# Banded attention in tiles of 32 queries by 64 keys, feeding a top-1 mixture of experts

## The chip, the cores and the metric

The kernel runs on one core of a Trainium2 chip. A core has a matrix engine (PE, TensorE; its weight loads are listed apart as PEld), three engines for elementwise work (DVE = VectorE, ACT = ScalarE, POOL = GpSimd), a queue engine that issues most DMAs (SP = SyncE) and 16 DMA engines. The metric is the device time of one execution in microseconds (us); lower is better.

## The reference

```python
B, H, S, D = 8, 8, 576, 64
scores = scale * q @ k.transpose(0, 1, 3, 2)
rel = pos[:, None] - pos[None, :]
mask_plain = (rel >= 0) & (rel < 32)                       # heads 0-3
mask_dil = (rel >= 0) & (rel < 128) & (rel % 4 == 0)       # heads 4-7
attn = softmax(where(mask, scores, -1e9))
x = (attn @ v).transpose(0, 2, 1, 3).reshape(4608, 512)
# top-1 mixture of 8 experts, gate logits with a bias per modality
logits = x @ w_gate + modality_bias[modality_id]
e_idx, gate_w = argmax(logits), softmax(logits)[e_idx]
out[e_idx == e] = gate_w * (relu(x @ w1[e]) @ w2[e])       # w1: 512x1024, w2: 1024x512
```

Every query looks at 32 keys: heads 0 to 3 at the last 32 positions, heads 4 to 7 at every fourth of the last 128. Everything is float32.

## The kernel before

**Two halves.** The first is attention with routing, the second the experts. Attention goes over 8 batches of 5 steps each, 40 steps (`s`, with `b, n = s // 5, s % 5`). Heads 0 to 3 are "plain" (`kd == 0`); heads 4 to 7 are "dilated" (`kd == 1`) and their positions are sorted into four classes of 144, so that their mask becomes a band of 32 too. Steps `n` = 0 and 1 take dilated tiles, 3 and 4 plain ones, 2 the rest of both and half as much.

**A tile before** is 64 queries (`TQ`) by 96 keys (`KW = TQ + WIN`); a step holds two tiles one above the other in the 128 partitions, for 2 values of `x`, 2 of `g` and 2 of `a`: 8 units of 128 rows. What a step does is spread over five turns of the loop, so that one turn `s` contains `scores` of step s (PE: `qT` x `kT` into the PSUM tile `pss`; DVE adds the mask at L397 and takes the row maximum at L399; POOL subtracts it in `sm`), `exp` of step s-1 (ACT, L404), a copy of values `shift_v` (ACT, L150 or L152), `attend` of step s-2 (PE, L418, into `po`), `logits` of s-4 (PE, L470 or L473 and L475), `normalize` of s-2 (DVE, L425 to L432), `turn` of s-3 (PE transposes at L456, ACT copy `ux`), a piece of `qk_chunks` for coming steps (PE transposes of q and k at L353, ACT copy into `qkT` at L355), `probsT` of s-1 (PE transposes of the probabilities at L410, ACT copy `pT` at L412), and `keep` of s-2 (DMA of the result `x_sb` to `x_dram`).

**Values** lie in three buffers `vw` of 96 partitions: 64 partitions of a block of 64 positions, and above them the 32 positions before, which `shift_v` copies from the block before.

**Order.** PE, DVE, ACT and SP run exactly in the order in which the loop issues (`manual_schedule`), and POOL in the order of its wrapper `pool`; each engine waits by itself for what its next instruction needs. SP issues, in that same order, the loads of q, k and v for the next batch, the stores of `keep` and the loads for the experts. `background` runs the routing of a finished batch (`gating`, the scatter of token numbers into `table` by POOL's indirect DMAs) in small pieces between the steps, on a time `state['t']` of 9 ticks a batch. After batch 2, four expert slots are already full: `fetch_slot` has SP read their token numbers into `idt`, and POOL gathers their rows of `x_dram` into `xr` (indirect DMAs, four to a slot) at ticks that a list names.

**PSUM** has 8 banks: `po` 2, `pss` 2 and a ring of two tiles of 2 banks (`banks()`), which `qk_chunks`, `probsT`, `turn` and later the experts' first product take by turns. When `state['go']` is set, near the end of attention, `pss` is given up and the experts start: 18 slots of 256 tokens and one of 128, each with 8 pieces of w1 (L948) and w2 (L928), split on ACT and DVE into a high and a low part (L896, L897).

## Time and profile before

| | |
|---|---|
| Median of 3 runs | 685.75 us (683.57 to 688.63) |
| The profiled execution | 687.67 us; its span, first to last instruction, 685.9 us |
| Mean granted PE clock | 0.971 |
| Busy share of the span | PE 94%, PEld 82%, DVE 67%, ACT 62%, POOL 36% |
| First scores (L391) to last | 11.7 us to about 229 us |
| Experts | from about 238 us to 677 us |

A row of the timeline is start, length, engine, line, operation, tiles, count, and in brackets the idle time before it with what ended it. A row of groups gives count, then busy us and mean ns of one, then idle time before. A float32 matmul stands as two records in the trace where it isn't a transpose.

### The profile page before, as it was taken

Reading aid. Unit: us, or ns where it says so; the run is one execution under the profiler, and the core shown is the slowest. Engines: PE = TensorE matmul, PEld = TensorE weight load, DVE = VectorE, ACT = ScalarE, POOL = GpSimd, SP = SyncE. Lnnn points to the kernel's source line nnn. Section 1 sums busy time; section 2 is a strip of 40 time slices with the busy share of each in tenths; the row PEclk is TensorE's granted clock in tenths of the full one; section 3 lists DMA queues with packets and bytes.
Section 4 is the critical chain, followed back from the end, with each engine's and each line's share of the span. In section 5 each row is a group of like instructions: output and inputs, shape, how many; then the busy total and the mean of one; then the engine's idle time right before and its main releaser. Section 6 shows DMA issues by size and latency. Waiting matters only on the chain. (4 is left out here: it accounts for less than half of the span.)

```text
span 685.9 us, 17663 instructions
## 1 busy us (share of the span) xinstructions
PE 644.7 (94%) x6481; PEld 563.9 (82%) x6481; DVE 456.7 (67%) x967; ACT 428.7 (62%) x749; POOL 248.1 (36%) x300
## 2 busy tenths in 40 slices
PE   7899988996989898999999999999999999999994
PEld 4777877875777787899999999999999999999983
DVE  4666565772657666866776677667766776677652
ACT  3777968675787554566566656655666566656552
POOL 7333554544656553333242331333313231311110
PEclk9899999998999799999999999999999999999998
DMA  9886976868598843593963337823323335831550
GB/s 207 218 188 168 189 178 153 184 170 185 125 187 214 265 97 97 145 248 105 267 175 93 94 109 213 216 78 110 103 83 78 108 117 151 240 92 63 154 145 14
DMA packets 133630, 103.32 MB, mean 151 GB/s; under 512 B 67648, under 2 KB 111698, under 8 KB 133540
## 3 DMA queue, kind: packets, MB, share of 16 engines
q1 hardware_dynamic: 124964, 82.31, 47.5%
q0 software_dynamic: 8176, 19.26, 9.8%
q8 instruction: 52, 0.85, 0.5%
q10 hardware_dynamic: 400, 0.59, 0.3%
q14 instruction: 38, 0.31, 0.2%
HBM read 127.52 MB, written 29.39 MB: 229 GB/s over the span
## 5 line engine op out<-in xcount | busy, mean ns | idle before, releaser
L897 DVE TENSOR_TENSOR w2l<-w2q,w2h 128x512 fp32r<-128x512 f32 x152 | 104.9, 690 | 42.2 <-ACT w2h L896 33.9
L317 POOL DMA_INDIRECT xr<-x_dram,idt x74 | 81.9, 1107 | 109.7 <-DMA x_slot<-xr 76.9
L948 PE MATMUL pt<-xh,w1l 128*128 128x256 f32 (+1 forms) x420 | 119.3, 284 | 1.5 <-DVE w1l L897 1.5
L948 PE MATMUL pt<-xh,w1h 128*128 128x256 f32 (+1 forms) x420 | 119.5, 285 | 0.7 <-DVE hl L955 0.7
L948 PE MATMUL pt<-xl,w1h 128*128 128x256 f32 (+1 forms) x420 | 119.2, 284 | 0.0
L928 PE MATMUL py<-w2h,hh 128*128 128x512 f32 x296 | 117.8, 398 | 0.0
L928 PE MATMUL py<-w2h,hl 128*128 128x512 f32 x296 | 117.0, 395 | 0.0
L928 PE MATMUL py<-w2l,hh 128*128 128x512 f32 x296 | 116.2, 393 | 0.0
L954 ACT ACTIVATE hh<-pt 128x256 fp32r<-128x256 f32 (+1 forms) x105 | 39.8, 379 | 119.0 <-PE pt L948 119.0
L317 POOL DMA_INDIRECT out_dram<-ys,idt x37 | 39.5, 1069 | 205.5 <-ACT ys L931 129.6
L897 DVE TENSOR_TENSOR w1l<-w1q,w1h 128x512 fp32r<-128x512 f32 x152 | 104.2, 685 | 1.3 <-ACT w1h L896 1.3
L896 ACT CAST w1h<-w1q 128x512 fp32r<-128x512 f32 x152 | 94.5, 622 | 1.2 <-DVE hl L955 0.9
L896 ACT CAST w2h<-w2q 128x512 fp32r<-128x512 f32 x152 | 93.1, 612 | 0.0
L948 PEld LDWEIGHTS pt<-xh,w1h 128*128 128x128 f32 x420 | 80.9, 193 | 6.4 <-DVE hl L955 0.9
L948 PEld LDWEIGHTS pt<-xl,w1h 128*128 128x128 f32 x420 | 80.9, 193 | 3.9
L948 PEld LDWEIGHTS pt<-xh,w1l 128*128 128x128 f32 x420 | 80.8, 192 | 2.0 <-DVE w1l L897 2.0
L317 POOL TENSOR_TENSOR sm<-sm,nmx 128x768 f32<-128x768 f32 (+1 forms) x40 | 53.7, 1343 | 77.4 <-DVE den L425 36.6
L955 DVE SCALAR_TENSOR_TENSOR hl<-pt,hh 128x256 fp32r<-128x256 f32 (+1 forms) x105 | 43.7, 417 | 54.7 <-ACT hh L954 54.6
L397 DVE TENSOR_TENSOR sm<-pss,masks 128x768 f32<-128x768 f32 (+1 forms) x40 | 34.9, 873 | 57.4 <-PE pss L391 49.5
L928 PEld LDWEIGHTS py<-w2l,hh 128*128 128x128 f32 x296 | 55.8, 188 | 13.3
L418 PE MATMUL po<-vw,pT 96*64 96x65 f32 (+1 forms) x1216 | 56.7, 234 | 8.6 <-DVE t L540 3.5
L418 PEld LDWEIGHTS po<-vw,pT 96*64 96x64 f32 (+1 forms) x1216 | 46.2, 141 | 19.6 <-ACT ex L528 4.3
(181 smaller groups left out, 1220.4 us busy)
## 6 DMA issues: line engine op xcount, KB each, us to landing
w2q<-in_moe_w_dram SPq DMA_DIRECT2D x76, 512.0 KB
w1q<-in_moe_w_dram SPq DMA_DIRECT2D x152, 256.0 KB
x_slot<-xr SPq DMA_DIRECT2D x18, 512.0 KB
xg<-x_slot SPq DMA_DIRECT2D x72, 128.0 KB
x_dram<-x_sb SPq DMA_DIRECT2D x32, 256.0 KB
st<-in_k_dram SPq DMA_DIRECT2D x8, 576.0 KB
st<-in_k_dram SPq DMA_DIRECT2D x32, 144.0 KB
st<-in_q_dram SPq DMA_DIRECT2D x32, 144.0 KB
```

What stands on the lines that cost most here:

```text
L317: ins = tc.keep_in_program_order(getattr(nc.gpsimd, name)(*args, **kw))
L397: nc.vector.tensor_tensor(out=sm.rearrange("p (a x) w -> p a x w", a=2), in0=pss[:, :, 0:2 * nx * KW].rearrange("p a (x w) -> p a x w", w=KW),
L418: nc.tensor.matmul(out=po[r0:r0 + nr, x, o:o + D + 1], lhsT=self.pT[:, 2 * self.nx * a + 2 * x + g, r0:r0 + nr], rhs=self.vts[kd][:, blk, ...
L896: nc.scalar.copy(out=hi, in_=raw)
L897: nc.vector.tensor_tensor(out=lo, in0=raw, in1=hi.bitcast(F32), op=ALU.subtract)
L928: nc.tensor.matmul(out=py[u], lhsT=ht[:, us], rhs=wt, start=(f + n == 0), stop=(f + n == FC + 1))
L948: nc.tensor.matmul(out=ph, lhsT=wt[:, c, :], rhs=xt[:, c, 0:cols], start=(c + i == 0), stop=(c + i == KC + 1))
L954: nc.scalar.activation(out=hh, in_=ph, func=AF.Relu)
L955: nc.vector.scalar_tensor_tensor(out=hl, in0=ph, scalar=0.0, in1=hh.bitcast(F32), op0=ALU.max, op1=ALU.subtract)
```

## The change

Tiles become 32 queries by 64 keys. Four of them lie above one another in the 128 partitions and two (`x` = 0, 1) side by side, so that `sm` is 4 units of 128 x 128 instead of 8 of 128 x 96, one transpose of `probsT` turns the probabilities of two units, and the two halves of its 128 output partitions are multiplied with values of 64 partitions each. A step has 32 score matmuls of 32 x 64 and 32 of attend instead of 16 and 16. The value buffers get 128 partitions (a second, shifted copy, for tiles that start in the middle of a block), which doubles the shifts: four a batch stay on ACT, four go to DVE. `probsT` moves ahead of `normalize` and `turn`. The PSUM ring is replaced by tiles of their own: `pc` (2 banks) for `qk_chunks`, `pt` (1) for `probsT`, `px` (1) for `turn`; the experts get `ph0` and `ph1`, and `pt` and `px` after attention. After the first two steps, only n = 2 has two chunks of `qk_chunks`. The stores of `keep` become two for each full step, v has four small loads more a batch, and the loads of q and k come at n = 1 and n = 3 instead of n = 0 and n = 4. The ticks at which POOL gathers the first two slots change.

```diff
-KW = TQ + WIN
+KW = 2 * WIN
+VO = D + 2
+VBLK = 20
...
-    ring = [pspool.tile([P, 2, 512], F32, name=f"pt{i}") for i in range(2)]
+    pt = pspool.tile([P, 512], F32, name="pt")
+    px = pspool.tile([P, 512], F32, name="px")
...
+    pss, pc = (spool.tile([P, 2, 512], F32, name=name) for name in ("pss", "pc"))
+    ring, turn = [], [0]
...
-    vws = [avw.tile([KW, 4 * (HT + 1), VB], F32, name=f"vw{i}") for i in range(3)]
+    vws = [avw.tile([P, VBLK, VB], F32, name=f"vw{i}") for i in range(3)]
...
+    def shift_v(copy, b, kd, low, n):
+
+        t = vw(b, kd).rearrange("p k d -> p (k d)")
+        w = (2 + 2 * kd) * VB * low
+        r0 = WIN * (1 - low)
+        copy(out=t[r0:r0 + WIN, 8 * VB * n + w:8 * VB * (n + 1) + w], in_=t[P - WIN - r0:P - r0, 8 * VB * n:8 * VB * (n + 1)])
...
         def scores(self):
...
+                            to = pss[WIN * c:WIN * (c + 1), a, kw * g + KW * x:kw * g + KW * (x + 1)]
+                            nc.tensor.matmul(out=to, lhsT=qT[kd][ar, h, WIN * j:WIN * (j + 1)], rhs=kT[kd][ar, h, WIN * j:WIN * j + KW], start=True, stop=True)
...
         def probsT(self):
-            ptt = banks()
-            nx = self.nx
-            for j in range(4 * nx):
-                nc.tensor.transpose(out=ptt[0:KW, j // 4, P * (j % 4):P * (j % 4 + 1)], in_=self.sm[:, j, :], identity=ident)
-            self.pT = awk.tile([KW, 8, P], F32, name="pT", bufs=1)[:, 0:4 * nx]
-            nc.scalar.copy(out=self.pT.rearrange("p (k j) c -> p k (j c)", j=4), in_=ptt[0:KW, 0:nx])
+            kw = self.nx * KW
+            for h in range(4):
+                nc.tensor.transpose(out=pt[0:kw, P * h:P * (h + 1)], in_=self.sm[:, h], identity=ident)
+            self.pT = awk.tile([P, 4, P], F32, name="pT", bufs=1)[0:kw]
+            nc.scalar.copy(out=self.pT.rearrange("p h c -> p (h c)"), in_=pt[0:kw])
 
         def attend(self):
...
+            for a in range(2):
+                for g in range(2):
+                    for x, c, kd, j, hh in self.js:
+                        r = slice(TQ * x, TQ * (x + 1))
...
+                        nc.tensor.matmul(out=po[WIN * c:WIN * (c + 1), x, o:o + D + 1], lhsT=self.pT[r, 2 * a + g, WIN * c:WIN * (c + 1)],
+                                         rhs=self.vts[kd][r, blk, (D + 1) * a:(D + 1) * (a + 1)], start=True, stop=True)
...
-            t0 = (b + 2) * 9 + 6
-            yield from together(first_rows(0, (t0, t0 + 1, t0 + 9, t0 + 10, t0 + 11, t0 + 12, t0 + 14)), first_rows(1, (t0 + 18, t0 + 19, t0 + 26, t0 + 27)), first_slot())
+            t0 = (b + 2) * 9 + 12
+            yield from together(first_rows(0, (t0, t0 + 1, t0 + 9, t0 + 10, t0 + 11, t0 + 12, t0 + 14)), first_rows(1, (t0 + 14, t0 + 15, t0 + 18, t0 + 19)), first_slot())
...
+    SHIFTS = (((on_dve, 1, 0, 0),), ((on_dve, 1, 1, 0),), ((on_act, 1, 0, 1), (on_dve, 1, 1, 1)), ((on_act, 0, 1, 1),), ((on_act, 0, 0, 0), (on_dve, 0, 1, 0)))
...
         if 0 <= s - LAG:
             steps[s - LAG].logits()
+        if 0 <= s - 1 < NST:
+            steps[s - 1].probsT()
         if 0 <= s - 2 < NST:
             steps[s - 2].normalize()
...
-        if 0 <= s - 1 < NST:
-            steps[s - 1].probsT()
...
-            if n == 0:
+            if n == 1:
                 state['k', 0] = load_one(b + 1, 0, k)
                 state['qk', b + 1, 0] = load_one(b + 1, 0, q), state['k', 0]
-            elif n == 1:
                 state['v', b + 1, 1] = load_v(b + 1, 1)
+            elif n == 3 and b + 2 < B:
+                state['qk', b + 2, 1] = load_qk(b + 2, 1)
             elif n == 4:
-                if b + 2 < B:
-                    state['qk', b + 2, 1] = load_qk(b + 2, 1)
                 state['v', b + 1, 0] = load_v(b + 1, 0)
...
-    ring.append(po)
+    ring += [pt, px]
```

How this moves the order is shown at three places. The first is PE in one whole step, n = 0 of the second batch, from its scores up to the next step's; the sizes are those of one output, and xN counts equal instructions. Before:

```order
L391 MATMUL pss<-qkT_102 64x96 x16
L418 MATMUL po<-vw_104,pT 64x65 x16
L470 MATMUL po<-ux,wgs 32x2x64 x4
L456 MATMUL pt_80<-ident,x_sb 128x128 x2
L353 MATMUL pt_79<-ident,st 128x96 x8
L410 MATMUL pt_80<-ident,sm 96x128 x8
L353 MATMUL pt_79<-ident,st 128x96 x8
```

and now (L378 is scores, L406 attend, L469 logits, L395 `probsT`, L455 `turn`, L345 `qk_chunks`):

```order
L378 MATMUL pss<-qkT_103 32x64 x32
L406 MATMUL po<-vw_104,pT 32x65 x32
L469 MATMUL po<-ux,wgs 32x2x64 x4
L395 MATMUL pt<-ident,sm 128x128 x4
L455 MATMUL px<-ident,x_sb 128x128 x2
L345 MATMUL pc<-ident,st 128x96 x8
```

The probabilities' transposes have moved ahead of `turn` and are half as many, the matmuls of scores and attend are twice as many, and one of this step's chunks has gone to the next step.

The second place is POOL in the middle of the fifth batch's scatter, where the first slot's rows are gathered; the first row is the subtraction of step 25 (counted from 0). Before:

```order
L317 TENSOR_TENSOR sm<-sm,nmx 128x768
L560 DMA table<-pay,dst 41472x3
L317 DMA xr<-x_dram_85,idt 128x256
L317 DMA xr<-x_dram_86,idt 128x256
L560 DMA table<-pay,dst 41472x3
L317 TENSOR_TENSOR sm<-sm,nmx 128x768
L560 DMA table<-pay,dst 41472x3 x2
```

and now, from the same subtraction on:

```order
L310 TENSOR_TENSOR sm<-sm,nmx 128x512
L559 DMA table<-pay,dst 41472x3 x2
L310 TENSOR_TENSOR sm<-sm,nmx 128x512
L559 DMA table<-pay,dst 41472x3
L310 DMA xr<-x_dram_86,idt 128x256
L559 DMA table<-pay,dst 41472x3
L310 TENSOR_TENSOR sm<-sm,nmx 128x4x64
L310 DMA xr<-x_dram_87,idt 128x256
```

The first gather stands one subtraction later, and the second one more.

The third place is SP over one batch of stores and loads, from the last store of plain tiles on. Before:

```order
L446 DMA x_dram_85<-x_sb 128x2x256
L141 DMA vw_104<-in_v_dram 64x4x128 x2
L141 DMA vw_104<-in_v_dram 16x4x128
L141 DMA vw_104<-in_v_dram 48x4x128
L141 DMA vw_104<-in_v_dram 64x4x128
L141 DMA vw_104<-in_v_dram 32x4x128
L449 DMA x_dram_86<-x_sb 128x2x256 x2
L439 DMA x_dram_85<-x_sb 64x256
L442 DMA x_dram_86<-x_sb 32x2x128 x2
L121 DMA st<-in_k_dram 96x4x384
L121 DMA st<-in_q_dram 96x4x384
L137 DMA vw_105<-in_v_dram 64x9x64 x4
```

and now, from the stores of dilated tiles on to the loads that follow the next plain ones:

```order
L445 DMA x_dram_87<-x_sb 64x4x128 x4
L124 DMA st<-in_k_dram 96x4x384
L124 DMA st<-in_q_dram 96x4x384
L432 DMA x_dram_86<-x_sb 64x256
L435 DMA x_dram_87<-x_sb 32x2x128 x2
L141 DMA vw_106<-in_v_dram 64x8x64 x4
L144 DMA vw_106<-in_v_dram 64x2x64
L145 DMA vw_106<-in_v_dram 32x2x64
L144 DMA vw_106<-in_v_dram 64x2x64
L145 DMA vw_106<-in_v_dram 32x2x64
L440 DMA x_dram_86<-x_sb 4x32x256 x4
L121 DMA st<-in_k_dram 96x6x64 x4
```

A batch has 35 DMAs on SP instead of 27 (8 of them k and q of the plain heads, which before stood between two stores of L446 and now behind the four of L440), and the loads of dilated k and q (L124) stand ahead of two stores where they stood behind them.

More of the change, by code (lines that the diff above doesn't have):

```diff
@@ L48 @@
 VB = 2 * D + 2
+VO = D + 2
+VBLK = 20
+TQ = 64
 HP = S // 2
@@ L178 @@
         nc.tensor.matmul(out=po[:, 0], lhsT=warm[:, 0:P], rhs=warm, start=True, stop=True)
-    starts = [None, 0, CL - 2 * TQ]
-    kinds = [(1, 0), (1, 0), (0, 0), (0, 0), (2, 0), (0, 3)]
-    masks = cpool.tile([P, len(kinds), KW], F32, name="masks")
+    masks = cpool.tile([P, 7, KW], F32, name="masks")
     nc.gpsimd.memset(masks, 0.0)
-    def band(m, r0, nr):
-        mt = masks[r0:r0 + nr, m, :]
+    for c in range(4):
+        mt = masks[WIN * c:WIN * (c + 1), 1, :]
         nc.gpsimd.affine_select(out=mt, in_=mt, pattern=[[1, KW]], compare_op=ALU.is_ge,
@@ L389, in scores @@
+            sm = awk.tile([P, 4, 2 * KW], F32, name="sm")[:, :, 0:kw]
             nmx = awk.tile([P, 8, 1], F32, name="nmx")[:, 0:4 * nx]
-            for x, g, a, r0, nr, qs, ks, _, _, _ in sorted(self.js, key=lambda j: (-j[4], j[0], j[1], j[3], j[2])):
-                nc.tensor.matmul(out=pss[r0:r0 + nr, a, KW * (2 * x + g):KW * (2 * x + g + 1)], lhsT=qs, rhs=ks, start=True, stop=True)
-            if self.n == 3:
-                mask = masks[:, 0:4, :].rearrange("p (a x) w -> p a x w", a=1)
-            else:
-                m0 = (0, 4, 5, 0, 2)[self.n]
-                mask = masks[:, m0:m0 + 1, :].rearrange("p (a x) w -> p a x w", a=1)
@@ L397, in scores @@
-            nc.vector.tensor_tensor(out=sm.rearrange("p (a x) w -> p a x w", a=2), in0=pss[:, :, 0:2 * nx * KW].rearrange("p a (x w) -> p a x w", w=KW),
-                                    in1=mask.broadcast_to([P, 2, 2 * nx, KW]), op=ALU.add)
-            nc.vector.tensor_reduce(out=nmx[:, :, 0], in_=sm, op=ALU.max, axis=AX.X)
-            pool.tensor_tensor(out=sm, in0=sm, in1=nmx.broadcast_to([P, 4 * nx, KW]), op=ALU.subtract)
+            for x in range(nx):
+                for g in range(2):
+                    for _, c, kd, j, hh in self.js[4 * x:4 * x + 4]:
+                        for a in range(2):
+                            ar = slice(D * a, D * (a + 1))
+                            h = 2 * hh + g
+                            to = pss[WIN * c:WIN * (c + 1), a, kw * g + KW * x:kw * g + KW * (x + 1)]
+                            nc.tensor.matmul(out=to, lhsT=qT[kd][ar, h, WIN * j:WIN * (j + 1)], rhs=kT[kd][ar, h, WIN * j:WIN * j + KW], start=True, stop=True)
@@ new lines, in scores @@
+            m0 = (0, 5, 1, 3, 1)[self.n]
+            mask = masks[:, m0:m0 + nx, :].rearrange("p (a g x) w -> p a g (x w)", a=1, g=1)
+            nc.vector.tensor_tensor(out=sm.rearrange("p (a g) w -> p a g w", a=2), in0=pss[:, :, 0:2 * kw].rearrange("p a (g w) -> p a g w", g=2),
+                                    in1=mask.broadcast_to([P, 2, 2, kw]), op=ALU.add)
+            sv = sm.rearrange("p k (x w) -> p k x w", w=KW)
+            nv = nmx.rearrange("p (k x) o -> p k x o", k=4)
+            nc.vector.tensor_reduce(out=nv[:, :, :, 0], in_=sv, op=ALU.max, axis=AX.X)
@@ L426, in normalize @@
+            if self.n <= 2:
+                r = slice(TQ if self.n == 2 else 0, P)
+                for a in range(2):
+                    o = (D + 1) * a
+                    nc.vector.tensor_scalar(out=den[r, a:2 * nx:2], in0=pov[r, a:2 * nx:2, o:o + VO + 1:VO], scalar1=1e-9, scalar2=None, op0=ALU.add)
             nc.vector.reciprocal(out=den, in_=den)
             self.xs = xs = awk.tile([P, 2, 4 * D], F32, name="x_sb", bufs=3)
-            plain, dil = xs[:, 0:nx].rearrange("p x (g a d) -> p (x g) a d", g=2, a=2), xs.rearrange("p a (j d) -> p j a d", d=D)
@@ L1044 @@
             state['y'] = ctx.enter_context(tc.tile_pool(name="ps_y", bufs=2, space=PSUM))
+            hpool = ctx.enter_context(tc.tile_pool(name="ps_h", bufs=1, space=PSUM))
+            ring += [hpool.tile([P, 512], F32, name=f"ph{i}") for i in range(2)]
             moe = slots(NS, ids_of, ahead, hold)
-        pieces = []
         if s < NST:
@@ L1051 @@
             steps[s].scores()
-            if b + 1 < B:
+        pieces = []
+        if s < NST:
+            if s < 2:
+                plain = qk_chunks(0, *state['qk', 0, 0])
+                pieces = plain[0:2] if s == 0 else plain[2:]
+            elif n < 2:
+                pieces = plain[n + 1:n + 2]
+            elif b + 1 < B:
                 if n == 2:
@@ L1068 @@
             steps[s - 1].exp()
-        if s < NST and n:
-            shift_v(b, *((1, 0), (1, 1), (0, 1), (0, 0))[n - 1])
+        if b and n == 0:
+            shift_v(nc.scalar.copy, b - 1, 0, 0, 1)
+        if s < NST:
+            for copy, *move in SHIFTS[n]:
+                shift_v(copy, b, *move)
         if 0 <= s - 2 < NST:
```

170 lines of the change are left out of this document (72 added, 98 removed).

## The prediction

> **What bounds the kernel now.** First the busy time by stretches, one call with two whole batches of attention (each from the scores of one n = 3 to those of the next), one with a stretch of the start and one of the experts. Columns: stretch, length, busy us of PE, PEld, DVE, ACT and POOL with counts, granted clock, DMA share, GB/s.
>
> ```profile
> 53.60:80.00 26.40, 25.02 (x472) 20.71 (x471) 16.90 (x42) 21.40 (x28) 13.29 (x18) 1.00 0.78 185
> 80.00:106.50 26.50, 24.48 (x460) 20.17 (x459) 17.01 (x42) 20.41 (x27) 14.10 (x19) 1.00 0.79 174
> 20.00:40.00 20.00, 18.40 (x295) 15.40 (x294) 12.22 (x32) 14.93 (x19) 7.05 (x7) 0.83 0.72 183
> 300.00:320.00 20.00, 20.00 (x129) 18.10 (x128) 14.33 (x26) 12.46 (x27) 9.18 (x9) 1.00 0.67 185
> ```
>
> PE is never idle among the experts (20.00 of 20), and the change leaves their work alone: whatever attention gains or loses passes on to the end. In attention a batch takes 26.4 us, PE works 25.0 of them and idles 1.4; ACT, next, works 21.4. So attention is bound by PE as well, with little room under it. The waits of PE between 20 and 235 us (engine, line, releaser, total us, times, longest) say the same:
>
> ```profile
> PE pt L410 <- ACT ux L459: 6.5, 1, 6.5
> PE po L418 <- DVE t L540: 3.5, 5, 0.8
> ```
>
> One wait of 6.5 us stands out; the next is the gating of each batch, five times in all. The 6.5 us are followed up below.
>
> **PE's part.** The timeline of PE shows a step's pieces by their starts; the difference of two starts is what a piece costs.
>
> ```profile
> 95.77 0.88 PE L353 MATMUL pt<-ident,st 96*128 96x96 f32 x8
> 96.58 0.89 PE L391 MATMUL pss<-qkT 64*64 64x96 f32 x32
> 97.40 1.15 PE L418 MATMUL po<-vw,pT 96*64 96x65 f32 x32
> 98.48 0.30 PE L473 MATMUL po<-ux,wgs 128*32 128x32 f32 x4
> ...
> 85.74 2.00 PE L418 MATMUL po<-vw,pT 96*64 96x65 f32 x22
> 87.62 0.39 PE L470 MATMUL po<-ux,wgs 128*32 128x128 f32 x6
> ```
>
> Scores cost 0.82 us for 32 records (25.6 ns each), attend 1.08 us, but 1.88 us in the mixed step with its 64- and 32-row outputs, although it has 24 records. One matmul takes some 240 ns by the groups, so several run at once, in different parts of the array: four in scores (two halves of rows, two of columns), two in attend (96 rows leave only the columns). The new shape, 64 rows by 32 columns, would allow eight, but doubles the records to 64 a piece. The nearest rows to such small outputs are the logits of the mixed step and the transposes behind them:
>
> ```profile
> 190.95 0.33 PE L473 MATMUL po<-ux,wgs 128*32 128x32 f32 x8
> 191.06 0.28 PE L475 MATMUL po<-ux,wgs 128*32 128x32 f32 x8
> 191.27 0.65 PE L456 MATMUL pt<-ident,x_sb 128*128 128x128 f32 x4
> 191.76 1.04 PE L410 MATMUL pt<-ident,sm 128*96 128x128 f32 x8
> 192.73 1.01 PE L391 MATMUL pss<-qkT 64*64 64x96 f32 x24
> ```
>
> Eight records of 32 columns pass in 0.11 us (191.06 less 190.95), 13.75 ns each; all sixteen up to the next kind in 0.32 us, 20 ns each, which counts the change of kind. Eight transposes take 0.97 us, 0.121 each.
>
> With r for the cost of one record, a full step changes by 128 r - (0.82 + 1.08) - 4 x 0.121, and the mixed step by 64 r - 1.88 - 0.62 (its 24 score records at 25.6 ns). A batch is four of the one and one of the other: 576 r - 12.0 us. Three values:
> - eight at once, all rounds kept: scores are now 8 rounds in 0.82 us, so 64/96 of 0.103 for a round of 64 moving columns; attend is 16 rounds in 1.08, so 0.0675 a round. A full step then has 0.55 + 0.54 us, the mixed one 0.27 + 0.54: -6.8 us a batch;
> - r = 13.75 ns: -4.1 us, PE at 20.9 us a batch;
> - r = 20 ns: -0.5 us.
> I take the middle one. It is nearest in columns, and it is a pace of issue, where the first asks that nothing but the array counts. The point from which PE gains nothing is r = 20.9 ns.
>
> What the moves of PE's order cost I set at nothing. `probsT` comes up to 2 us earlier in the step; by the lengths below its `sm` is ready 3.0 us after its scores (mask 0.69, maximum 0.69, POOL about 1.0, exp 0.63), and with steps of 4.5 us PE gets to it some 5.5 us after them. If those 2.5 us of cover go, PE waits for exp. Two chunks through one `pc` at n = 2 must wait for ACT's copy between them (0.99 us, L355 below), but that is the step whose attend gets shortest.
>
> **The other engines**, from the groups of the same two batches (count, busy, mean ns); the memset is from the groups of the whole run:
>
> ```profile
> L412 ACT COPY pT<-pt 96x1024 f32<-96x1024 f32 x8 | 8.1, 1009 | 1.6 <-PE pt L410 1.6
> L412 ACT COPY pT<-pt 96x512 f32<-96x512 f32 x2 | 1.2, 588 | 0.0
> L404 ACT ACTIVATE sm<-sm 128x768 f32<-128x768 f32 x8 | 6.7, 841 | 0.1
> L404 ACT ACTIVATE sm<-sm 128x384 f32<-128x384 f32 x2 | 1.1, 526 | 0.0
> L355 ACT COPY qkT<-pt 128x768 f32<-128x768 f32 x10 | 9.9, 986 | 0.6 <-PE pt L353 0.5
> L152 ACT COPY vw<-vw 32x1040 f32<-32x1040 f32 x4 | 4.2, 1057 | 0.1
> L397 DVE TENSOR_TENSOR sm<-pss,masks 128x768 f32<-128x768 f32 x8 | 7.6, 954 | 10.1 <-PE pss L391 8.2 <-ACT qkT L355 1.9
> L397 DVE TENSOR_TENSOR sm<-pss,masks 128x384 f32<-128x384 f32 x2 | 1.1, 558 | 1.5 <-PE pss L391 1.5
> L425 DVE TENSOR_SCALAR den<-po 128x8 f32<-128x8 f32 x8 | 1.3, 160 | 1.3 <-PE po L470 0.9 <-PE po L475 0.4
> L432 DVE TENSOR_TENSOR x_sb<-po,den 128x512 f32<-128x512 f32 x8 | 5.5, 691 | 0.3
> L317 POOL TENSOR_TENSOR sm<-sm,nmx 128x768 f32<-128x768 f32 x8 | 11.8, 1470 | 17.4 <-DVE den L425 11.4 <-PE po L470 3.6 <-DVE nmx L399 1.5
> L163 DVE MEMSET vw<- 32x520 f32 x2 | 1.0, 492 | 0.3
> ```
>
> ACT: `pT` falls from 1009 to 588 ns in four steps (-1.7 us), exp from 768 to 512 elements, by the slope of the two rows to 631 ns, and to 421 in the mixed step (-0.95); four shifts before, four now. 21.4 becomes 18.8. DVE: mask and maximum fall to 690 ns in four steps and by 0.14 in the fifth, both alike (-2.4); four more `den` (+0.6), one product less in the mixed step (-0.4, an estimate from its half size), and four shifts of 1040 elements: not shown on DVE, between nothing and ACT's 1057 ns each; I take two memsets of 520, 0.98 us (+3.9). 16.9 becomes 18.6. If DVE's cover fails, it is `po`: the shift stands between the row maximum and `den` on DVE, and the next attend waits for `normalize` behind it; with 0.69 + 0.69 + 0.98, two `den` of 0.16, a reciprocal (about 0.2) and 0.69 that is 3.6 of a step of 4.5. POOL's subtraction falls in proportion, from 1.47 us to about 1.0.
>
> SP has more to do: 35 DMAs a batch instead of 27. Its queue over one batch (start, length, line, tiles, count), and the length of one by source (min/median/max ns):
>
> ```profile
> 54.60 4.66 SPq L141 DMA_DIRECT2D vw<-in_v_dram  x6
> 59.35 0.90 SPq L449 DMA_DIRECT2D x_dram<-x_sb  x2
> 62.53 0.49 SPq L439 DMA_DIRECT2D x_dram<-x_sb  x1
> 63.11 1.01 SPq L442 DMA_DIRECT2D x_dram<-x_sb  x2
> ...
> 65.21 4.96 SPq L137 DMA_DIRECT2D vw<-in_v_dram  x4
> 70.26 1.28 SPq L446 DMA_DIRECT2D x_dram<-x_sb  x1
> ...
> 78.43 1.32 SPq L446 DMA_DIRECT2D x_dram<-x_sb  x1
> L137 SPq DMA_DIRECT2D vw<-in_v_dram x32: 586/636/3067, 13.1 to 212.8; - x32
> L446 SPq DMA_DIRECT2D x_dram<-x_sb x16: 381/568/2423, 44.3 to 254.4; - x16
> ```
>
> From 54.60 to 79.75 it issues 27 DMAs and idles 2.28 us (60.25 to 62.53): 22.9 us, 0.85 each. Part of that is not issue: four loads of L137 took 4.96 us where the shortest take 0.59 each, and two stores of L446 2.60 where the shortest take 0.38, in a burst where k, q and v of both kinds follow one another. The eight new ones are small; at 0.5 us (L442's pair took 1.01) they add 4.0. So SP needs between 22.4 (22.9 + 4.0 less the 2.6 and 1.84 of those two lines) and 26.9 us. The change pulls the burst apart, so I stay near the lower end.
>
> **Sum for a batch.** PE 20.9 plus the 1.4 that it idles now is 22.3; SP's lower end is 22.4; I take 22.5, a gain of 3.9 us. The bytes are nearly the same, so the DMA rate would rise from 185 to some 217 GB/s. The ends are 20.0 (PE at 18.2, ACT at 18.8, plus waits) and 26 (SP near its upper end; beyond it lies the second rival).
>
> **The stall.** POOL's row, with what it waited for, and the scores some microseconds later:
>
> ```profile
> 159.40 1.07 POOL L317 DMA_INDIRECT xr<-x_dram,idt  x1 [6.05 <-DMA idt<-table]
> 170.17 1.56 PE L391 MATMUL pss<-qkT 64*64 64x96 f32 x32
> ```
>
> POOL waited 6.05 us for the token numbers of the first slot, then issued two gathers in a row, with the next subtraction of `sm` queued behind them; exp, `probsT` and PE's 6.5 us follow, and then a step at half pace (1.56 against 0.89 us). Now the first gather stands one subtraction later and the second another one later, so the load has some 4.5 us more. But SP reaches that load later too, behind four more loads of v. I take 5.5 us gained, between nothing and 8.
>
> **Total.** Seven batches at 3.9 are 27.3; the first one, which waits for its loads, 2 (0 to 3.9); the stall 5.5: 34.8 us. The profiled execution took 687.67 us (span 685.9 and 1.8 around it), 1.9 above the median: 652.9 on its scale, 651 against the median.
>
> **The rivals.**
> - *Records cost what they cost now* (slower). If r stays at 25.6 ns, a batch gets 576 x 0.0256 - 12.0 = 2.7 us longer: 8 x 2.7 - 5.5 = +16, **702**. It decides from 20.9 ns. Against it stand the 13.75 ns of L473. The Trainium skill, TensorE: Matmul & The Clock Gate, section "Wait — 56ns, not 53.3ns?", says that starts of small matmuls never come closer than about 25 ns. By that rule this rival would hold; the rows of L473, which run in separate column strips, do not agree. 5%.
> - *SP sets the pace* (slower). At 0.85 us each, 35 DMAs are 29.8 us, +3.4 in each of six batches that load for the next, less the stall: +15, **701**. It decides from 26.4/35 = 0.75 us. For it: SP issues 22.9 of 26.4 us already. Against: most of the excess is waiting on the same bytes. 7%.
> - *The clock drops* (no change). Between 20 and 40 us PE was busy 18.40 of 20 and the clock still only 0.83. With more engines near 20 us a batch, PE waits more often; at 0.83 its 20.9 becomes 25.2, plus 1.4: as now, and only the stall is won: **680**. The Trainium skill's same page, Part 1, has the clock fall after an idle window of about 3.4 us. By that rule nothing would change here, since no such wait is left; the row of 20 to 40 us, with 1.6 us idle in all, does not agree. 10%.
> - *The eight-fold case* (faster still): 20.0 a batch, 7 x 6.4 + 3.9 + 8 = 56.7, **629**. 6%.
>
> **The numbers.** The forecast, up to 668 us, holds 68%; the slow end of PE or SP, where a batch takes 25 to 26 us and part of the stall goes (668 to 683), 4%. The range of 630 to 683 takes in all bounds and leaves out the two slower rivals and half of the eight-fold case. A measurement here tells about 1% from no change. Faster by over 1% (below 679): 68 + 6 + 4 and a little of the clock's case, 0.79. Within 1%: 0.09. Slower: 0.12, the two rivals.
>
> **What would show it.** Scores and attend by their starts near 0.9 us each (right), near 0.55 (eight at once) or 1.6 (first rival). A batch between two n = 3 scores at 22 to 23 us. SP without a pause and `x_sb` waiting for `x_dram` would be the second rival; a clock under 0.95 in the batches the third. No wait of POOL for `idt` above 2 us. The experts from their third slot on must look as they do now; if they don't, the forecast is wrong in a way that I haven't priced.

## The result, and the profile after

The changed kernel is slower: 724.74 us median (721.13 to 731.05) against 684.76 for the kernel before on the same chip, a ratio of 1.058, with a 95% interval of 1.050 to 1.067. The forecast was 651, its range 630 to 683. The profiled execution took 731.05 us, its span 729.3.

Where the time comes from is seen in one step: the last mask add of attention (timeline of VectorE: start, length, line; L397 of before, L381 of after).

```profile
229.77 0.94 DVE L397 TENSOR_TENSOR sm<-pss,masks 128x768 f32<-128x768 f32 x1
```

```profile
274.84 0.69 DVE L381 TENSOR_TENSOR sm<-pss,masks 128x512 f32<-128x512 f32 x1 [0.47 <-PE pss L378]
```

It comes 45.1 us later, and the span is 43.4 us longer: all of the loss is in attention. This start is the yardstick of the experiments below. Now 140 us of attention of before, the same of after, and 20 us of after's experts (length, busy us of PE, PEld, DVE, ACT, POOL with counts, granted clock, DMA share, GB/s).

```profile
60.00:200.00 140.00, 124.19 (x2254) 103.39 (x2255) 84.51 (x225) 101.50 (x129) 71.96 (x95) 0.96 0.76 171
```

```profile
60.00:200.00 140.00, 102.65 (x3184) 87.37 (x3182) 77.99 (x240) 82.51 (x121) 59.63 (x82) 0.85 0.68 146
340.00:360.00 20.00, 20.00 (x129) 18.14 (x129) 14.47 (x27) 12.25 (x25) 10.85 (x10) 1.00 0.83 208
```

The experts are as before. In attention every engine now has air: PE idles 37 us of 140 instead of 16, all others work less, and the clock fell to 0.85. So no engine is the bound. The waits of PE between 20 and 285 us say more (total, times, longest):

```profile
PE po L406 <- issue: 16.1, 10, 4.1
PE po L507 <- DVE lT L488: 11.4, 3, 10.2
PE pc L345 <- ACT qkT L347: 8.8, 7, 1.3
PE pss L378 <- ACT qkT L347: 6.9, 8, 1.0
PE po L534 <- DVE oh L526: 6.4, 5, 1.4
PE pss L378 <- issue: 6.2, 6, 3.6
PE pc L345 <- issue: 6.0, 2, 4.3
...
PE po L469 <- issue: 2.2, 2, 1.8
```

Waits "for issue" are waits for nothing that the profile shows. Two of them on PE's timeline:

```profile
106.02 0.88 PE L378 MATMUL pss<-qkT 64*32 64x64 f32 x64
107.28 0.35 PE L406 MATMUL po<-vw,pT 64*32 64x65 f32 x16 [0.38 <-DVE dstf L493]
111.38 0.97 PE L406 MATMUL po<-vw,pT 64*32 64x65 f32 x48 [3.75 <-issue]
...
140.96 0.75 PE L406 MATMUL po<-vw,pT 64*32 64x65 f32 x50
145.50 0.47 PE L406 MATMUL po<-vw,pT 64*32 64x65 f32 x14 [3.79 <-issue]
```

PE stops in the middle of one attend, after 16 of its 64 records in one case and after 50 in the other, and goes on 3.8 us later. The profile shows nothing that these records wait for, but the count of instructions fits. Number PE's weight loads and matmuls through from the start: the eight such waits of over 1.5 us stand before instruction 1473, 1729, 3009, 3777, 4545, 6081, 7617 and 9153, and each of these numbers leaves 193 over a multiple of 256. With the shorter ones, down to 0.3 us, it is 17 waits between the first mask add and the last: 15 at 193, 29.3 us together ("waits at 193" below), and two of 0.4 us elsewhere. Before has two at 193, 2.0 us: 98.83 to 99.57 and 189.30 to 190.57. The DMA view (queue, kind: packets, MB, share of 16 engines) shows what comes in 256s. Take the wait that starts at 107.63. First the stretch from 103.8 to 108.3 us, then that from 108.3 to 109.8:

```profile
q1 hardware_dynamic: 719, 1.07, 98.5%
```

```profile
q1 hardware_dynamic: 1022, 0.37, 114.0%
q8 instruction: 1, 0.02, 5.1%
```

A packet of instructions (16 KB, so 64 bytes for each of 256) starts at 108.40, 0.8 us into the wait, lands at 109.62, and PE goes on 1.8 us later. For 4.5 us before it the 16 engines were full of loads and stores and no such packet passed. All 15 waits end in this way, 1.3 to 1.8 us after the landing of the packet that brings the instruction at which PE stopped. PE had issued all that it held and **ran out of instructions**. The Trainium skill, Runtime: NRT & Kernel Launch, section "Instruction fetch mechanics", has instructions come in blocks of 256 through a DMA queue, which the trace shows; it also has that hidden because the sequencer is slower than the refill. That doesn't hold here: 64 weight loads and 64 matmuls of scores pass in 0.88 us.

A second sign is the second rival's: `x_sb` waits for the stores of its last use, where before had 0.4 us of this (waits of VectorE, 20 to 285 us):

```profile
DVE x_sb L423 <- DMA x_dram<-x_sb: 13.7, 6, 9.5
```

Later comparisons were made on several chips; on some of them the kernel before itself takes some 722 us, so ratios to it, not times, are compared across them. The yardstick comes from one profiled execution, which can lie some microseconds beside the median (731.05 against 724.74 for after, 670.34 against 679.17 in experiment 5); where it and the ratio differ, the ratio counts.

### The profile page after: what moved, and what is told of

It is laid out like the page before. It is cut to its first block, busy times and chain, and to the rows that moved or that the text cites. A ratio compares the mean times of both kernels' runs of the same rounds, so it can differ in the third digit from the quotient of the medians.

```text
span 729.3 us, 21857 instructions
## 1 busy us (share of the span) xinstructions
PE 631.7 (87%) x8529; PEld 556.1 (76%) x8529; DVE 455.4 (62%) x1019; ACT 406.5 (56%) x749; POOL 246.1 (34%) x313
## 5 line engine op out<-in xcount | busy, mean ns | idle before, releaser
L947 PE MATMUL ph<-xh,w1l 128*128 128x256 f32 (+1 forms) x320 | 91.0, 284 | 1.8 <-DVE w1l L896 1.8
L947 PE MATMUL ph<-xh,w1h 128*128 128x256 f32 (+1 forms) x320 | 91.4, 286 | 0.1
L947 PE MATMUL ph<-xl,w1h 128*128 128x256 f32 (+1 forms) x320 | 90.7, 283 | 0.0
L953 ACT ACTIVATE hh<-ph 128x256 fp32r<-128x256 f32 (+1 forms) x80 | 30.4, 380 | 99.4 <-PE ph L947 99.4
L310 POOL TENSOR_TENSOR sm<-sm,nmx 128x512 f32<-128x512 f32 (+1 forms) x40 | 48.6, 1214 | 86.6 <-DVE nmx L385 51.8
L345 PE MATMUL pc<-ident,st 96*128 96x96 f32 x384 | 52.4, 290 | 24.6 <-ACT qkT L347 12.3
L381 DVE TENSOR_TENSOR sm<-pss,masks 128x512 f32<-128x512 f32 (+1 forms) x40 | 25.3, 633 | 73.5 <-PE pss L378 69.9
L347 ACT COPY qkT<-pc 128x768 f32<-128x768 f32 (+1 forms) x56 | 48.7, 893 | 39.3 <-PE pc L345 39.2
L397 ACT COPY pT<-pt 128x512 f32<-128x512 f32 (+1 forms) x40 | 23.4, 584 | 82.6 <-PE pt L395 74.7
L345 PEld LDWEIGHTS pc<-ident,st 96*128 96x128 f32 x384 | 46.5, 173 | 26.5 <-ACT qkT L347 14.4
L947 PEld LDWEIGHTS ph<-xh,w1h 128*128 128x128 f32 x320 | 61.5, 192 | 4.5 <-ACT w1h L895 0.5
L947 PEld LDWEIGHTS ph<-xl,w1h 128*128 128x128 f32 x320 | 61.4, 192 | 3.2
```

Of the source, the lines that this page charges most:

```text
L310: ins = tc.keep_in_program_order(getattr(nc.gpsimd, name)(*args, **kw))
L345: nc.tensor.transpose(out=to[:, w], in_=inn, identity=ident[:PQ, :PQ])
L347: nc.scalar.copy(out=dst, in_=src)
L381: nc.vector.tensor_tensor(out=sm.rearrange("p (a g) w -> p a g w", a=2), in0=pss[:, :, 0:2 * kw].rearrange("p a (g w) -> p a g w", g=2), i ...
L397: nc.scalar.copy(out=self.pT.rearrange("p h c -> p (h c)"), in_=pt[0:kw])
L947: nc.tensor.matmul(out=ph, lhsT=wt[:, c, :], rhs=xt[:, c, 0:cols], start=(c + i == 0), stop=(c + i == KC + 1))
```

## The experiments

**1. Wide records in after**, in the four full steps; attend is changed in the same way:

```
-                    for _, c, kd, j, hh in self.js[4 * x:4 * x + 4]:
+                    for _, c, kd, j, hh in self.js[4 * x:4 * x + 4:1 if self.n == 2 else 2]:
...
+                            nr = WIN if self.n == 2 else 2 * WIN
+                            to = pss[WIN * c:WIN * c + nr, a, kw * g + KW * x:kw * g + KW * (x + 1)]
```

> The kernel after, with its scores and attend issued in records of 64 queries instead of 32 in the four full steps of a batch (32 records each instead of 64, of the same 64 keys; the second 32 queries of each record get the window of the first, so their attention is another one, and some tokens go to other experts). DMAs, PSUM tiles, shifts and the order of the program stay. Four records of 64 x 64 fit beside one another where eight of 64 x 32 did, so PE's work should stay within 0.1 us a step; what halves is the number of instructions. Theory 1, PE runs out of instructions (it gets them in packets of 256, two ahead, and the packet comes late behind the loads): the seven or so idle stretches of PE of 3.6 to 4.3 us that end with nothing the profile shows go, and the last mask add, at 274.8 us after and 229.8 before, comes at 225 to 240; with the experts unchanged the time is 675 to 690. Theory 2, SP's 35 DMAs a batch set the pace: the last mask add stays at 270 to 278 and the time at 720 to 730. Theory 3, the one chunk buffer and the new order of PE cost it: as theory 2.

Ratio 1.047 (1.041 to 1.054), last mask add at 264.1. The waits at 193 fell from 29.3 us to 7.7 in 4, and yet little was won: all three theories missed. What stands in their place is a wait of VectorE (60 to 285 us; in after it is 13.7):

```profile
DVE x_sb L425 <- DMA x_dram<-x_sb: 35.2, 15, 8.2
```

**2. Narrow records in before**: as many PE instructions as after, attend split like scores.

```
+                for d in range(0, nr, WIN):
+                    nc.tensor.matmul(out=pss[r0 + d:r0 + d + WIN, a, KW * (2 * x + g):KW * (2 * x + g + 1)], lhsT=qs[:, d:d + WIN], rhs=ks, start=True, stop=True)
```

> The kernel before, with each score and attend record of 64 queries split into two of 32: the same work and the same results, 64 records instead of 32 in each, so as many PE instructions as after; DMAs, PSUM ring, shifts and order are those of before. Theory 1 (PE runs out of instructions): waits of 3 to 4 us of the kind of after appear, some 1 to 2 a batch; the last mask add moves from 229.8 to 250 to 275 us and the time from 685 to 705 to 730. Theory 2 (SP's 35 DMAs) and theory 3 (chunk buffer, order): nothing changes, 680 to 690, since neither is touched.

Ratio 1.046 (1.040 to 1.053), last mask add at 264.8. Only the matmuls changed, cut into twice as many of half the width, and before loses 4.6%. Its timeline and PE's waits:

```profile
72.50 1.17 PE L420 MATMUL po<-vw,pT 96*32 96x65 f32 x63
76.44 0.24 PE L420 MATMUL po<-vw,pT 96*32 96x65 f32 x1 [2.78 <-issue]
```

```profile
PE po L420 <- issue: 15.9, 7, 3.3
PE pss L392 <- issue: 7.2, 5, 3.0
```

63 of 64 records of one attend pass, the last one 2.78 us later. 17 waits of this kind, 16 at 193 over a multiple of 256 and one at 195, take 31.0 us, and PE's idle time in attention grows by 29.5 of the 35.0 lost. **This is the first limit, shown by itself.**

**3. 27 DMAs a batch in after**; the stores of n = 0 and 1 are joined like those shown, and the last line is that of v's last rows:

```
-                for x in range(2):
-                    queue.dma_start(out=rows[x], in_=xs[:, x])
+                queue.dma_start(out=x_dram[0][r0:r0 + 2 * P, :].rearrange("(u p) f -> p u f", p=P), in_=xs)
...
-            for g in range(2):
+            for g in range(2 if b == 0 else 0):
```

> The kernel after with the 27 DMAs a batch of before: each full step's rows are stored by one DMA instead of two (into other rows of the buffer, so that tokens' rows are exchanged), and the four small loads of v's last rows are made for the first batch alone. Bytes are the same but for those rows. Theory 1 (PE runs out of instructions): a little sooner at best, since the packets then wait behind fewer transfers: last mask add at 262 to 275, time 712 to 726. Theory 2 (SP's DMAs): 35 instead of 27 was all the trouble, so the last mask add comes back to 225 to 240 and the time to 675 to 690. Theory 3 (chunk buffer, order): unchanged, 720 to 728.

Ratio 1.039 (1.030 to 1.048), last mask add at 257.7, the waits at 193 still 35.9 us: as the first theory had it, a little better than its bound.

**4. No loads of q, k and v from the third batch on**:

```
+            if b + 1 > 1 and n in (1, 4):
+                state['qk', b + 1, 0] = state['qk', 1, 0]
```

> The kernel after without the loads of q, k and v for the batches from the third on: they work on the tiles of the second one, and v on what its buffers hold, so their attention is another one and tokens go to other experts; the time of the end then depends on how many slots the experts need, and the last mask add is what counts. PE's instructions, PSUM tiles and order stay. Theory 1 (PE runs out of instructions because the packets wait behind the loads): from the third batch on a packet comes about 2 us after it could be asked for, as among the experts, instead of 4 to 7, the idle stretches of 3.6 to 4.3 us go, and a batch takes 21 to 24 us: last mask add at 215 to 235. Theory 2 (SP's queue): the same, as SP has 14 DMAs a batch left, so this run doesn't part 1 from 2. Theory 3 (chunk buffer, order): 31 to 34 us a batch as after, last mask add at 265 to 278.

Last mask add at 234.8, ratio 1.004 (1.001 to 1.008); waits at 193 fall to 15.5 us, and a batch takes 27.3 us, not the 21 to 24 expected.

```profile
60.00:200.00 140.00, 110.72 (x3701) 93.66 (x3701) 91.58 (x276) 93.90 (x139) 73.53 (x100) 0.94 0.23 54
```

So even with the DMA engines a quarter full PE idles 29 of 140 us: for instructions, for the chunk buffer, for the gating. PE's own work per batch is 110.72 / (140 / 27.3) = 21.6 us.

**5. Both diffs, 1 and 3.**

> Both edits of the two earlier runs at once: records of 64 queries (half of the PE instructions in scores and attend of the full steps; second windows wrong, so tokens go to other experts) and 27 DMAs a batch (joined stores, v's last rows loaded for the first batch only). Alone they brought the last mask add from 274.8 us only to 264.1 and 257.7. Theory A, two limits of nearly the same pace lie on each other, the instructions of PE and the queue of SP (whose late stores keep x_sb occupied: 35.2 us of waits of DVE in the run with wide records): with both gone a batch takes 23 to 26 us, last mask add at 212 to 235. Theory B, a third thing sets the pace (the single chunk buffer with 1.3 + 0.9 us a batch, the gating with 1.4, the clock): 31 us a batch stay, last mask add at 245 to 262.

Ratio 0.983 (0.977 to 0.989), last mask add at 217.7, batches of 25.4 us in the mean. By the yardstick the edits won 10.7 and 17.1 us alone and 57.1 together; by the ratio 1.1 and 1.9% of before's time alone and 7.6% together. **Two limits of nearly the same pace lay on each other**, and each hid what removing the other would bring. With both away the time is 1.7% under before's. The forecast was 5%, and the batch is still 2.9 us longer than its 22.5, so part of the miss lies in neither limit.

**6. The stores on another queue**:

```
-            steps[s - 2].keep(nc.sync)
+            steps[s - 2].keep(nc.scalar)
```

> The kernel after with the stores of x (nine a batch) issued from ScalarE's queue instead of SP's; nothing else changes, and the result is the reference's. SP then has 26 DMAs a batch, ACT nine issues of some 0.5 us more. Theory A (instructions and SP's queue both): the waits of x_sb go, the instructions stay the limit: last mask add at 252 to 265, time 705 to 718, like the run with 27 DMAs. If SP's queue were all: 225 to 240, 675 to 690. If ACT's 4.5 us a batch more hurt as much as SP gains: 270 to 280, 720 to 730.

Last mask add at 261.2, as expected, but the end came no sooner: ratio 1.058 (1.051 to 1.064). The experts' first matmuls waited 6.9 us for slot 0's weights, and the 150th record of their first layer starts at 324.9 us instead of 325.8.

**7. The first chunk right behind the scores**, beside edit 6:

```
+        if pieces:
+            pieces[0]()
         if 0 <= s - 2 < NST:
             steps[s - 2].attend()
```

> The stores on ScalarE's queue as in the run before, and the first (or only) chunk of q and k of a step issued on PE right behind the scores instead of at the step's end, so that its copy out of the one chunk buffer is over before the second chunk or the next scores need it. Result as the reference's. These two waits are 1.26 and 0.92 us a batch, 17 us in all. If PE's instructions are the limit, what is saved there is waited elsewhere: 0 to 6 us less than the run before, last mask add at 247 to 265. If the waits themselves are on the path, 12 to 17 us less, last mask add at 238 to 250.

Last mask add at 260.4, ratio 1.058 (1.051 to 1.066): nothing gained. Waits for the chunk buffer fell from 8.8 to 3.0 us, and those at 193 rose from 17.6 to 28.0.

**8. q and k loaded in large pieces, arranged by POOL.**

```
+            queue.dma_start(out=raw.rearrange("p (h x) -> p h x", h=4), in_=src[b, 0:4].rearrange("h (p s) d -> p h (s d)", s=SI))
...
+        for s0 in (0, SI // 2):
+            pool.tensor_copy(out=tv[:, s0:s0 + SI // 2], in_=rv[:, s0:s0 + SI // 2])
```

> The kernel after, with q and k of the plain heads (from the second batch on) loaded by one DMA of 1536-byte pieces each instead of four of 256-byte pieces, and put into the order that the transposes need by POOL (two copies of 96 x 768 for each tensor, at n = 2 and n = 4). SP has 29 DMAs a batch instead of 35, and loses those that take 1.14 us each; PE's instructions and the result are those of after. Theory A (instructions of PE and SP's queue, each with 31 to 32 us a batch): SP's limit falls to about 21 us a batch and the instruction packets wait behind fewer transfers, so a batch takes 26 to 29 us, last mask add at 230 to 255, time 685 to 710. If the packets' wait hangs on the number of transfers above all, nearer the lower end. Against it: POOL's four copies (1 to 1.5 us each, an estimate from its 1.04 to 1.46 us for 128 x 512) may hold up the subtraction of the row maximum: then 255 to 270 and 710 to 725.

Ratio 1.049 (1.043 to 1.056): about 1% won, the less favourable case of the expectation; PE waited 11.3 us for POOL's copies.

**9. The same with the early chunk of 7**, the same lines moved:

> The kernel of the run before, with the first chunk of a step issued right behind the scores. The waits for the one chunk buffer, 1.26 + 0.92 us a batch, go. With SP's limit gone and the instructions the only one left, 0 to 6 us less than the run before; if PE's own work is what is left, 12 to 17 us less: 670 to 695.

Ratio 1.063 (1.056 to 1.070), a miss: PE now waited 26.0 us for POOL.

**10. Wide records, stores on ScalarE's queue**, the diffs of 1 and 6 together:

> Records of 64 queries as in the first run (half of PE's instructions in scores and attend; second windows wrong, so tokens go to other experts), and the stores of x from ScalarE's queue: SP has 26 DMAs a batch, but every load, every byte and every store of after is still made. It tells SP's queue from the number of transfers in the run with both edits (last mask add at 217.7 us; with the wide records alone 264.1). Theory A, the queue: the waits of x_sb for x_dram are gone and a batch takes 24 to 27 us, last mask add at 217 to 238. Theory B, the DMA engines, which have as many and as small transfers as after: 250 to 264.

Last mask add at 257.6, ratio 1.055 (1.048 to 1.062): theory A fell. The waits of `x_sb` are gone, but SP's now read

```profile
SPq L141 <- DMA x_dram<-x_sb: 31.9, 8, 7.1
```

Loads of v, which touch no `x`, wait for stores of x on another queue. In the trace of this run eight semaphores serve both queues in turn, and each such DMA waits for its own from the use before, whichever queue that was on. So a slow store holds up what follows, wherever it is issued.

**11. All shifts on ScalarE**: in `SHIFTS` each `on_dve` becomes `on_act`.

> The kernel after with all value shifts on ScalarE, as before: undoes one part of the change. DVE loses four copies of 0.70 us a batch, ACT gains four of 1.06. If neither engine sets the pace (the instructions and SP's queue do), the time stays within 1% of after's: 718 to 730 on its scale, ratio to before 1.048 to 1.068. If DVE's shifts held up den and the next attend: 5 to 20 us less.

Ratio 1.051 (1.044 to 1.058): within the bounds of "no pace". But the last mask add came at 264.2, 10.6 us sooner, as in experiment 1, and the intervals overlap with after's. So the shifts are not the main part of the loss; whether they cost up to 1% is open.

**12. Only the scores narrow, in before**: the two lines shown for 2, and nothing in attend.

> The kernel before with only the score records split into 32 queries each; attend stays. Same work and results; PE's instructions go from some 945 a batch to some 1220, half way to the 1490 of the run with both split (last mask add at 264.8 us against 229.8, ratio 1.046). Theory: a packet of 256 instructions takes about 5 us to come under the loads, so the supply lasts for 256 in 5 us, 1220 in 24 us, under the 26.4 that a batch takes: only where instructions crowd do waits come, ratio 1.003 to 1.02. If instead each instruction had a price of its own, half of the loss would show: ratio 1.02 to 1.027.

Ratio 1.031 (1.024 to 1.037), above the first expectation; the second, up to 1.027, lies inside the interval. Waits at 193 take 11.4 us in 6, so the mean rate, which the expectation put under the supply, does not protect the bursts. The rest of the 19 us by which the last mask add moved (248.8) I have not traced.

**13. Number or form of the DMAs?** Experiment 5 with eight small loads a batch added, four of them by

```
+            for i in range(4 if b else 0):
+                nc.sync.dma_start(out=tiny[:, 4 + i], in_=v[b, 0:1, 0:2].rearrange("o s d -> o (s d)"))
```

> The run with wide records and 27 DMAs a batch (last mask add at 217.7 us, batches of 22 to 28), with eight loads of 512 bytes a batch put in where the eight DMAs were taken out, so 35 again with the bytes and pieces of 27; nothing reads what they load. Second windows are wrong as in that run and tokens go to other experts. Theory A, the number of DMAs: every one waits until the one eight places before it has landed, and takes its place behind the others in the engines, so 35 take a third longer than 27: 28 to 32 us a batch, last mask add at 245 to 265. Theory B, the bytes and small pieces (512-byte stores, v's last rows): SP only has eight issues of 0.4 us more, 217 to 228.

Ratio 0.981 (0.975 to 0.987): nothing lost. The number of DMAs is not the second limit; theory A fell.

**14. Wide records and joined stores**, v's loads as in after: the diffs of 1 and 3 without the last two lines.

> Wide records (second windows wrong, tokens go to other experts) with joined stores, in pieces of 1 KB as before, and all loads of v's last rows: 31 DMAs a batch. Theory A, the number of DMAs: between the 264.1 of 35 and the 217.7 of 27, last mask add at 228 to 252. Theory B, pieces: if the 512-byte stores are what costs, 217 to 226; if the loads of v's last rows are, 252 to 264.

Ratio 0.985 (0.979 to 0.991). So joining the stores is enough to take the second limit away. What is wrong with them stands in the DMA view, after from 117.3 to 119.3, while four stores of n = 4 are under way, and run 14 from 103.6 to 105.3, in such a place:

```profile
q1 hardware_dynamic: 201, 0.19, 27.9%
...
st<-in_k_dram SPq DMA_DIRECT2D x2, 144.0 KB
x_dram<-x_sb SPq DMA_DIRECT2D x1, 128.0 KB
```

```profile
q1 hardware_dynamic: 555, 0.46, 79.0%
```

27.9% of 16 engines are 4.5. The store's pattern is `"(c x q) f -> x c q f"`, four blocks of 32 rows with the four outermost, and it runs on about four engines; the loads of k issued behind it hardly start in these 2 us. The Trainium skill, DMA: Bandwidth & Descriptors, section "Why a DMA increments its semaphore by 16 and not by 1", says that a DMA uses the largest number of engines, up to 16, that divides the size of the outermost dimension on both of its sides. By that rule four engines are used, and the trace agrees: 4.5.

**15. Wide records, the stores of n = 3 and 4 spread**: the rows land where they belong, with 32 rows outermost:

```
+                for c in range(4):
+                    rows = x_dram[0][r0 + 2 * P * (n - 3) + TQ * c:r0 + 2 * P * (n - 3) + TQ * (c + 1), :]
+                    queue.dma_start(out=rows.rearrange("(x q) f -> q x f", x=2), in_=xs[WIN * c:WIN * (c + 1)])
```

> Wide records (second windows wrong, tokens go to other experts), and of the stores only those of the plain heads' full steps (n = 3 and 4) changed: four of 32 rows each, with the 32 rows as the outermost of the transfer, instead of two with four blocks outermost. Right rows, same 1 KB pieces, 39 DMAs a batch. In the trace of after the 512 pieces of four such stores pass in 7 us, some 43 in half a microsecond at 0.05 us each, so through about four of the 16 engines; the joined ones pass at 110 to 165 in half a microsecond. Theory A, stores that use four engines are the second limit: as with the joined stores, ratio 0.975 to 0.99, in spite of 39 DMAs. Theory B, the 512-byte pieces of the dilated stores: nothing gained over the wide records alone, ratio 1.035 to 1.05.

Ratio 1.015 (1.009 to 1.021), between the two theories: about half of the way from 1.047 to 0.985. So the shape of these stores is part of the second limit, and this run does not show what the rest is.

**18. With the stores of n = 0 and 1 joined as well**, as in 3:

> Wide records and spread stores of n = 3 and 4 as in the run with ratio 1.015, and now also the stores of n = 0 and 1 joined into one of 1 KB pieces (their halves of rows then land in other rows, so the experts compute on exchanged rows; second windows are wrong as before). 37 DMAs a batch. Theory A, the 512-byte pieces of the dilated stores are the rest of the second limit: ratio 0.975 to 0.99, like the run with all stores joined. Theory B, the spread stores themselves cost (eight issues a batch instead of two, 32 rows each): 1.005 to 1.02, nothing gained.

Ratio 1.017 (1.012 to 1.022): the 512-byte pieces of the stores of n = 0 and 1 don't matter. Stores of 32 rows are still slower than those of 128; while they pass, the DMA view from 110.3 to 112.5 has

```profile
q1 hardware_dynamic: 370, 0.28, 47.7%
```

Why they don't fill 16 engines is open. A rival is their issue: in this run SP took 4.65 us for the eight stores around this place, one of 64 KB every 0.58 us or 113 GB/s, and the view's 0.28 MB in 2.2 us are 127 GB/s, so the engines may have had no more to do. No run parts the two.

**16. After with the spread stores only**, the diff of 15 without that of 1:

> The kernel after with only the stores of n = 3 and 4 spread in that way; result as the reference's. The instructions of PE are left as the limit: as in the run with 27 DMAs, ratio 1.03 to 1.045 against 1.058 of after. If the instructions only waited because the stores were in the way, 0.98 to 1.0.

Ratio 1.036 (1.029 to 1.043), as expected with the instructions left.

**17. The same with two heads' scores in one matmul:**

```
+    kz = [aper.tile([P, 2 + 2 * kd, 2, WIN + (S, HP + 4)[kd]], F32, name=f"kz{kd}") for kd in range(2)]
...
+                        nc.tensor.matmul(out=to, lhsT=qT[kd][:, h, WIN * j:WIN * (j + 1)], rhs=kz[kd][:, h, :, WIN * j:WIN * j + KW], start=True, stop=True)
```

> The kernel after with the spread stores and with the scores of two heads in one matmul: k lies in a tile with zeros beside it (rows of one head, columns of the other), so 128 rows by 32 queries give both heads' 64 keys; result as the reference's. PE's instructions fall from 1446 to some 1160 a batch, scores' records to 32 a step, each twice as long. k's copy is split by rows, one half to VectorE (about +3 us a batch there, +1.5 on ScalarE), and the chunks use three PSUM tiles in turn. If a packet of 256 instructions needs 5 us, 1160 need 22.6: PE's own 21 to 23 us and waits of 1 to 3 then make a batch of 23.5 to 26, last mask add at 215 to 230 where before has 229.8, ratio 0.975 to 1.0. If the instructions still crowd too much in a step: ratio 1.0 to 1.025.

Ratio 1.025 (1.020 to 1.030), at the end of its less favourable case. PE's instructions fell to 1158 a batch and the waits at 193 to 5.0 us in 4; waits for VectorE's copies of k, 13.9 and 5.3 us, came instead. So after, run 16 and this one, which all leave the computation whole, stand at 1.058, 1.036 and 1.025; no version of that kind beats the kernel before.

## Why the prediction was wrong, step by step

- **The failed step is "Sum for a batch": "PE 20.9 plus the 1.4 that it idles now".** Its 20.9 holds: 21.6 us of PE's work with the loads away (experiment 4). The 1.4 does not: in after PE idles 37.35 of 140 us, 8.7 a batch of 32.8. The step took it that what was idle before stays idle, and that more instructions come for nothing. 2048 more matmuls, each with its weight load, raised a batch from some 940 to some 1450 instructions; waits for them took 29.3 us in attention instead of 2.0, and experiment 2 shows that this alone costs before 4.6%. The two waits of this kind in before, 0.73 and 1.28 us, were there to be read as a limit close by. Waits behind the slow stores came on top (under SP). With both away a batch takes 25.4 us, not 22.5: there PE still waits 10.2 us for the gating, 8.8 and 6.8 for the chunk buffer and 7.8 for exp in the whole of attention. What each of these costs was not tried.
- **r, the cost of a record**: right. Within an attend of after the median distance of two records is 14.3 ns, within scores 11.5 (before: 30.2 and 20.9); 13.75 was forecast. By their starts an undisturbed scores takes 0.66 us and an attend 0.78 at the least, where some 0.9 was named as the sign. So the first rival, with its rule of 25 ns, is out.
- **SP**: "so I stay near the lower end" was wrong. Between 60 and 200 us SP spent 120.5 us on 148 DMAs, 0.81 each: past the 0.75 from which the second rival decides, with the waits of `x_sb` that it named. But its price was put on the number of issues, and experiment 13 shows that, beside joined stores, eight more cost nothing. The eight new DMAs were called small; what counted was the shape of the four at n = 3 and 4.
- **The clock**: the third rival's sign appeared, 0.85. PE's work was 102.65 / (140 / 32.8) = 24.0 us a batch, 2.4 more than in experiment 4, at a clock of 0.94. The clock stood at half for 104 of the 258 us between the first mask add and the last, in before for 19 of 217. It falls behind the waits (last section); what it costs by itself was not tried.
- **"What the moves of PE's order cost I set at nothing"**: two chunks through one `pc` and the scores behind the last chunk wait 8.8 + 6.9 us in after. Experiment 7 took most of it away and nothing was won, while the waits at 193 grew by 10.4 us: the instructions were the limit there. What it costs with both limits away is not shown.
- **The other engines**: near. From the groups of 60 to 200 us:

```profile
L310 POOL TENSOR_TENSOR sm<-sm,nmx 128x512 f32<-128x512 f32 x18 | 22.9, 1275 | 37.4 <-DVE den L420 13.4 <-DVE nmx L385 13.1 <-PE po L469 7.5
L158 ACT COPY vw<-vw 32x1040 f32<-32x1040 f32 x18 | 19.0, 1057 | 0.4
L381 DVE TENSOR_TENSOR sm<-pss,masks 128x512 f32<-128x512 f32 x18 | 12.3, 686 | 26.7 <-PE pss L378 25.2 <-issue 1.0
L158 DVE COPY vw<-vw 32x1040 f32<-32x1040 f32 x17 | 11.8, 695 | 0.5
```

  The mask add takes 0.69 us as said, a shift 0.70 on VectorE where 0.98 was taken, POOL's subtraction 1.28 where "about 1.0" was.
- **The stall**: "no wait of POOL for `idt` above 2 us" was wrong. Its first gather still stands behind a long wait:

```profile
185.49 1.07 POOL L310 DMA_INDIRECT xr<-x_dram,idt  x1 [7.39 <-issue]
```

  The profile names no releaser, but SP issued the load of `idt` only at 182.25, behind the loads of v, it landed at 184.69, and the gather followed 0.8 us later. What went is PE's wait of 6.5 us for it. In its place PE waits 4.3 us at 249.7 for `sm`, whose subtraction stood behind a gather of POOL that had waited 13.1 us for `x_slot<-xr`, and 10.2 us near the end (L507, behind VectorE's `x_sb` and the stores). So the 5.5 us were not kept.
- **The rivals were taken one at a time.** The signs of two of them, SP's and the clock's, came together with a limit that was not on the list. SP's had another cause than the one priced, and the clock's share is not known. Experiment 5 shows why no single limit would have given the time.

## What to carry to other kernels

When a change cuts matmuls into smaller ones, count PE's instructions per microsecond as well as its busy time, and look in the profile of before for waits "for issue": here 256 in 7.2 us (some 940 in 26.4) left 2.0 us of such waits in attention, and as many in 5.8 us (some 1450 in 32.8) 29.3 us. When a change alters the pattern of a store, look at its outermost dimension; with four blocks outermost it ran on about four of 16 engines. When removing one suspect wins little, remove two at once before dropping either: here 1.1 and 1.9% made 7.6%.

## What was not expected of the hardware

- PE's instructions come in packets of 256, and when they run out a wait of up to 4.3 us follows. No packet of attention started before PE was 235 instructions into the block two before it, so no more than about two blocks are at hand. Among the experts, where PE takes some 20 us for a block, most started 216 to 250 instructions into it; beside the loads of attention five started only after PE had stopped.
- A 128 KB store with four blocks outermost ran on 4.5 of 16 DMA engines, and for 2 us the loads queued behind it hardly used the others; later they did so in bursts.
- The granted clock falls to half behind waits of some 4 us, and stays there for 6.8 to 10.2 us behind the four longest of them. In after, the wait from 46.39 to 50.47 us and what follows it:

```profile
47.00:50.40 3.40, 0.00 (x0) 0.00 (x0) 0.95 (x2) 0.00 (x0) 1.46 (x1) 0.85 1.31 202
50.50:57.00 6.50, 5.58 (x133) 4.93 (x137) 2.19 (x7) 3.58 (x5) 0.00 (x0) 0.50 0.40 87
```
